# Rearranging the first 605 entries of a hand-kept instruction order (attention, token mixing, weight conversion)

## Chip, cores and metric

One Trainium2 chip, one of its cores. The metric is device time in microseconds (us), the median of the runs shown; lower is better.

## The reference

For a batch of 4, 8 heads, 576 positions and a head width of 64 the reference computes three stages one after another, all in float32 accuracy:

```
out_d     = softmax(scale * q_d k_d^T) v_d        # q, k, v averaged over 4 neighbours: 144 positions
out_local = softmax(scale * q k^T, |i-j| < 4) v   # a band of 7 keys
x  = repeat(out_d, 4) + out_local                 # heads side by side: 4 x 576 x 512
u  = x + (relu(x^T w_tok1) w_tok2)^T              # token mixing, hidden width 256
u  = u + relu(u w_ch1) w_ch2                      # channel mixing, hidden width 1536
th = u w_theta;  y = w_tok_r (u cos th) + w_tok_i (u sin th)
out = (u + y) + relu((u + y) w_ch)
```

The weights come as 64-bit floats and are converted on the chip.

## The kernel before, in words

Products are made exact enough by splitting a float32 value into a high part (rounded by ScalarE, ACT) and a low part (the rest, by VectorE, DVE), and adding three TensorE (PE) products (lines 135 to 139). A 64-bit weight is turned into these two parts by `converted` (lines 146 to 198): a DMA of the raw words, two ACT operations (L173, L174), three DVE operations (L176 to L186), an integer add on GpSimd (POOL, L190), the rounding on ACT (L192) and the subtraction on DVE (L194).

Nothing orders the work of attention, token mixing, channel mixing and conversion but one list, `ORDER` (lines 30 to 69). Each name in it is a generator, and each entry runs that generator to its next `yield`, which emits the instructions of one step:

```python
with tc.manual_schedule(engines={act.engine, dve.engine, pool.engine, pe.engine, nc.sync.engine}):
    for e in ORDER:
        name, _, times = e.partition("*")
        for _ in range(int(times or 1)):
            next(gens[name], None)
```

So the list fixes, for every engine and for the one queue of SyncE (SP) that issues all DMAs, the order of its own instructions. Between engines only data and buffers make one wait for another. In this text a step is written with its number from 0: F0:6 is the seventh entry F0. The names:

- **P n**: DMA of queries and keys of head pair n (16 pairs, 582 KB, tile qk, four buffers). **K n**: DVE, the sums over four neighbours (L368, L369). **W n**: four DMAs of the pair's values, tile vw, two buffers (L334). **V Q**: DMA of the values of a quad (two pairs), then three POOL sums (L345, L348, L351).
- **L n**: banded attention of a pair. L:0 PE mask (pairs 0 to 3 begin with 24, 12, 12 and 12 filler products, L280), L:1 PE scores (L480), L:2 DVE maximum and subtraction (L492, L493), L:3 ACT exponent, L:4 PE transposes (L505), L:5 ACT copies, L:6 PE product with vw (L515), L:7 DVE division into x (L529).
- **F Q**: pooled attention of a quad. F:0 PE scores (L381, needs K of both pairs), F:1 DVE maxima (L399, L407), F:2 ACT exponents, F:3 PE transposes (L424, L429), F:4 ACT copies, F:5 PE product (L440 to L447, needs V), F:6 DVE division (L451 to L454), F:7 two DMAs of the result to DRAM (tile od, L457), F:8 three DMAs back, four times over (tile xu, L463, L466).
- **A n**: DVE adds xu to x (L542). **T Q**: token mixing of a quad. T:0 ACT high part, T:1 DVE low part (L553), T:2 ACT, T:3 and T:4 PE first product, T:5 to T:8 PE second product. **E** and **U** take these products out of PSUM (U's last step writes uT to DRAM).
- **G0 to G6**: conversion of the token mixing's weights, six steps (DMA, ACT, DVE, POOL, ACT, DVE); T0:3 needs G0 to G2, T0:5 needs G3 to G6. **X0 to X7**: the same for the first third of the channel weights. **C i**: channel mixing of 384 positions: DMA of uT, ACT, DVE, then PE in eight steps of 12 products, C:3 to C:6 (first product, needs X0, X1, X4, X5) and C:7 to C:10 (second, needs X2, X3, X6, X7), with **H** and **O** taking them out. **I**: the constants.

The scores, transposes and products of L and F share two wide PSUM buffers, so a step that takes one waits until an earlier one is read.

Of the kernel before, what the change touches and what calls it, by code (L numbers as in the profile page):

```python
# [27 lines left out]


ORDER = """  # L30
G3 P0 G2 I*2 P1 G3 P4 G3 V0 P2 G3 K0 G3 G2 I G2 I L0*2 P3 K1 F0 W1 L0 F0 L1 L0 G3 F0 V0 L1*2 P5 V0 L2 W0 G2 K2 V0 G2
F0 G1 L1 V1 F0 L2 K3 G0 G6 K4 L0 F0 L0 L2 L1 G2 F1 L2 K5 L1 L0 F1 G1*2 F1 F0 V1 W3 L0 F1 G5 G0 L1 F0 G0 F1 G6 F2 L1
G0 P6 W2 G5 G6 L3 V1 F2 F0 V1 L3 G6 F2 F1 L3 G1 G4 F1 L2 P7 L5 L2 K6 L5 F1 G1 L3 A0 V2 X0 A1 L3 G1 T0 L5 G0 T0 L2 G2
F1 L3 G0 G4 F2 G5 T0*2 V2 X2 L2 G6 W5 F2 K7 V2 L4*2 E0.0*2 T0 L4 V3 V2 A2 L3 E0.1 L5 G4 L4 W4 L5 G6 L5 G4 L3 X2 F3
G5 P8 P9 A3 G4 F2 G5 E0.1 T1 G4 G5 T0 F2 V3 L4 F3 F2 T0 L4 V3 X2 F3 L6 V3 L6 X7 T0 P11 L6 X2 X0 F3 K8 U0.0 L6 T0 X2
X0 U0.0 F3 L4 U0.0 V4 K9 F2 F3 X0 L6 L4 L6 T1 F4 U0.1 X0 F3 T1 L5 U0.1 X0 T1 U0.1 F4 X7 X4 V4 F3 T1 X7 F4 W6 L5 X7
E1.1 F4 E1.0 E1.1 L8 V4 L8 X7 E1.0 X1 A4 F4 T1 P10 A5 T1 X2 T2 L8 T1 U1.0*2 T2 T1 U1.0 X1 F3 L7 X7 L7 T2 X1 T2 X4 X5
K10 X1 L8 L6 U1.1*2 L7 T2 E2.0 U1.1 W7 X4 L7 V4 X1 L7 F4 W9 L7 L6 X4 E2.1 E2.0 C0 E2.1 T2 X1 L8 K11 X5 L7 T2 X5 L8
W8 L9*2 L7 X5 P13 T2 P12 L9 L10 C0 A6 F5 X4 C0 U2.0 L10 U2.0 X5 U2.0 C0 X3 F5 X6 F4 F5 C0 A7 F4 L10 T3 X4 F5 L9 V5
T3 H0.1 L8 U2.1 F5 T2 H0.1 H0.0 K12 T3 L9 U2.1 X5 C0 L9 U2.1 K13 F4 X6*2 L10 T3 X3 W13 H0.0 X6 H0.2 F6 E3.0*2 V5 P14  # L40
T3 F6 V5 H0.2 F6 C0 V6 V5 L8 X3 E3.1 L9 H0.3 F5 E3.1 X3 W10 L9 F6 X3 F5 L10 V6 A9 T3 F5 T3 V6 U3.0 L10 K14 T3 V6
U3.0 X6 U3.0 T3 H0.3 X3 X6 L11*2 C0 L11 P15 U3.1*2 A8 F6 U3.1 C0 F5 T4 L11 L12 L10 O0.1 K15 C0 C1 W11 L10 O0.0 C0
T4*2 F7 O0.3 O0.2 L12 C1 O0.3 T4 L12 F7 L12 T4 C1 L11 E4.1 F6 L11 F7 L11 F6 C1 A10 W12 E4.0 L11 F6 F7 E4.0 A11 F7
L12 E4.1 C1 H1.0 T5 C2 F6 L13*2 H1.1 L12 H1.1 T4 T5 T4 U4.0 L13 C1 U4.0 H1.0 U4.0 L13 V7 T4 H1.2 T5 L13 L15 L13 T4
U4.1 L12 U4.1 L15 L12 W15 V7 C1 H1.2 A12 V7 U4.1 T5 H1.3 V7 H1.3 L13 E5.0 C1 L13 F7 C1 F7 E5.0 F7 L15 L14*2 A13 L15
C1 O1.0 L14 F7 O1.1 L14 T5 W14 C1 E5.1 C2 E5.1 T6 L14 L15 L14 T5 T6 T5 U5.0 C2 T5 U5.0 L15 U5.0 T5 O1.2 T6 O1.3*2
L15 L14 T6 U5.1 L14 U5.1*2 L15 T6 E6.0 A14 A15 C2 E6.1 C3 E6.0 T7 E6.1 T6 T7 H2.0 T6 U6.0 H2.0 T7*2 U6.0*2 C3 T6*2
T7 U6.1*2 E7.0 U6.1 C2 E7.1*2 E7.0 T7 H2.1*2 T7 U7.0 T7 U7.0*2 T7 C2*2 H2.2 U7.1 H2.2 U7.1 C3 U7.1 R0 X8 X17 H2.3
X11 H2.3 C2 X19 C2*2 X8 O2.1 X8 C2 O2.2 X8 O2.0 X11 C3 O2.3*2 X21 C3 H3.0 X19 H3.0 X19 X8 C3 X17 X8 X17 C4 H3.1 C3
H3.2*2 X17 H3.1 X19 X20 H3.3 X21 H3.3 C3 X11 X9 C3 C4 O3.0 X21 X17 X19 C3 C4 X21 C3 O3.2 X11 X21 X13 C4 O3.3 O3.1  # L50
X21 O3.3 X12 X17 X9 C4 X9 X20 X19 C4 X9 H4.0 X13 H4.0 X20 C5 C4 X15 H4.2 H4.1 X9 H4.1 X20 H4.2 H4.3 B2 X16 H4.3 C4
X9 X13 C4 C5 X13 X20 C4 O4.1 X12 X10 C5 X13 C4 O4.2 X12 B2 C5 O4.0 X12 X11 X13 C5 O4.3 H5.0 X20 X16 O4.3 X23 B2 C5
H5.1 X10 H5.0 X10 C5 H5.2 X12 X11 X10 H5.1 B2 H5.3 X14 X10 H5.3 J0 H5.2 X16 C5 M2.4 X23 X10 X16 X23 X15 C5 X18 C5
O5.1 X23 X22 B2 O5.2 O5.0 X12 X15 X14 C5 X23 X14 X16 M2.5 B2 O5.3 X14 X16 O5.3 R1 B2 X15 X40 X23 X18 X30 M2.6 B2 X18
M2.5 X18 B2 M2.8 X22 M2.8 X35 X22 M2.7 B2 X15 X14 M2.4 X22 M2.6 M2.9 X18 M2.7 B2 X15 X22 X33 X14 X40 X18 X40 X30 B0
X22 M2.10 X40 M2.11 M2.9 M2.11 M2.10 B2 X40 X36 X30 X35 B2 X35 X30 B0 X33 B0 X35 X24 B2 X33 X35 X38 X30 X40 X33 B0
X30 X28 B0 X38*2 X36 B0 X36 X38 X33 B2 X35 M0.4 X36 X39 X28 M0.4 X28 X29 X38 B0 X38 X28 B0 M0.7 X27 M0.5 X36 M0.5
M0.6 M0.7 X28 X36 B0 X39 M0.6 X39 M0.8 B0 X29 X33 X39 X28 M0.9 B0 M0.10 X27 M0.8 M0.9 M0.10 M0.11 B1 X27 X24 X37
X39*2 M0.11 B0 X24 B0 X24 B1 X27 X34 B1 X27 X25 B0 X24 N0.0 X27 X29 X34 N0.0 X29 B0 X34 X25 X31 X24 B1 N0.3*2 X25
N0.3 B1 M1.4 N0.1 X25 M1.4 N0.2 B1 X34 N0.3 M1.5 X37*2 B1 N0.2 X37 N0.2 B1 M1.7 X25 M1.7 X37 X32 M1.5 X26 X29 N0.0  # L60
B1 M1.6 X29 M1.6 X37 N0.1 B1 M1.9 N0.1 X31 M1.9 X31 M1.8 B1 X34 X32 M1.8 X31 X25 M1.11 B5 M1.10 J1 X26 M1.10 M1.11
B1 X26 X32 X26 B1 B5 X32 X26 B5 X32 B1 N1.0 N1.1*2 N1.0 N1.1 B1 B5 N1.3 X26 N1.2 N1.3 B5 X34 N1.3*2 B5 M5.5 N1.0
M5.4 B5 M5.6*2 M5.5 N1.2 B5 M5.4 N1.2 J2 B5*2 M5.9 M5.7 X31 M5.7 M5.8 M5.9 B5 M5.8 M5.10 N2.0*2 N2.3 M5.11 B4 M5.10
M5.11 B5 N2.3 N2.1 N2.3 B5 B4*2 B5 X31 N2.1 N2.2 X32 R2 N2.3 N2.0 N2.1 B4*2 N2.2*2 B4 Z B5 M4.4 M4.5 M4.6*2 M4.4
M4.5 B4*2 M4.7 J4 B4 M4.8 B4 M4.9 ZS M4.9 M4.8 ZS B4 M4.10 M4.7 ZS M4.11 B3 M4.11 M4.10 B4*2 N4.0 B3 B4 N4.1*2 B3
N4.1 B4 N4.2*2 B3 N4.3*3 B3 N4.3 N4.2 B3 N4.0*2 B3 M3.6 M3.4 M3.5 M3.4 ZS J5 B3 M3.7 ZS M3.7 ZS*2 B3 M3.5 M3.8 M3.6
M3.8 B3 N5.3 N5.2 N5.3 N5.1 N5.3 B3 M3.10 N5.1 M3.9 M3.10 M3.9 N5.1 N5.0 M3.11*2 B3 N5.3 N5.2 ZS N5.2 N5.0 B3 J3
N5.0 B3 N3.0*2 N3.1 N3.0 B3 N3.1 N3.2 N3.1 N3.2*2 N3.3*4
""".split()
# [1029 lines left out]
```

## Time and profile before

| | us |
|---|---|
| median of 3 runs | 690.69 (686.81 to 691.47) |
| the profiled execution | 689.01 |
| its span, first to last instruction | 687.2 |
| PE busy | 663.0 (96% of the span) |
| DVE busy | 472.0 |
| granted clock of PE, mean | 0.989 of full |

The profile is of one execution. In the rows below, a row of instructions has start, duration, engine, line, operation, output and input, count, and in brackets how long the engine stood idle before it and what ended that. A row of a stretch has the stretch, its length, busy time of PE, PE's weight loads, DVE, ACT and POOL (with counts), the granted PE clock, the mean busy share of the DMA engines and GB/s.

### The profile page before, as it was taken

The numbers are of one execution on the slowest core, as the hardware profiler recorded it, in microseconds if no ns is written. First come the engines' busy times: TensorE is split into PE (matmuls) and PEld (weight loads), VectorE is DVE, ScalarE is ACT, GpSimd is POOL, SyncE is SP. The second block draws the span as 40 slices with busy tenths as digits, with TensorE's granted clock in tenths as the row PEclk, the third lists the DMA queues.
The fourth block names the chain that finished last, engine by engine and source line by source line (L and its number), as shares of the span: only waits on it lengthen the run. The fifth ranks groups of instructions, "written<-read, shape, count | busy, mean of one in ns | idle before, by whom it ended". The sixth has DMA issues, their size and how long they took to land.

```text
span 687.2 us, 17270 instructions
## 1 busy us (share of the span) xinstructions
PE 663.0 (96%) x7368; PEld 634.5 (92%) x7368; DVE 472.0 (69%) x840; ACT 304.8 (44%) x594; POOL 96.8 (14%) x79
## 2 busy tenths in 40 slices
...
PEclk9979999999999999999999999999999999999999
...
GB/s 291 209 273 221 253 273 258 186 163 163 87 145 155 192 286 196 207 168 131 150 209 55 174 156 169 74 140 134 23 132 1 132 92 0 61 140 1 70 1 70
DMA packets 85612, 100.36 MB, mean 146 GB/s; under 512 B 44256, under 2 KB 65888, under 8 KB 85536
## 3 DMA queue, kind: packets, MB, share of 16 engines
...
q14 instruction: 18, 0.15, 0.1%
HBM read 74.34 MB, written 24.90 MB: 144 GB/s over the span
## 4 chain that ended last, share of the span: by engine, by line
PE 87%; DMA 5%; DVE 5%; ACT 1%; issue 1%; SPq 0%; POOL 0%; DVEq 0%; POOLq 0%; ACTq 0%
PE c L646 7%; PE c L138 7%; PE c L137 7%; PE c L649 7%; PE c L647 7%; PE c L139 7%; PE y L137 6%; PE y L138 6%; PE y L139 6%; PE th L138 2%; PE th L137 2%; PE th L139 2%; PE t L137 2%; PE t L138 2%; PE t L139 2%; PE o L515 1%
## 5 line engine op out<-in xcount | busy, mean ns | idle before, releaser
L190 POOL TENSOR_TENSOR ww<-ww,raw 128x512 int32<-128x512 int32 (+2 forms) x43 | 65.3, 1523 | 184.9 <-DVE ww L186 89.8
L662 ACT ACTIVATE g<-c 128x384 fp32r<-128x384 f32 x72 | 34.3, 492 | 105.0 <-PE c L139 89.9
L137 PE MATMUL y<-wrh,zh 128*128 128x288 f32 x256 | 75.0, 296 | 0.0
L138 PE MATMUL y<-wrl,zh 128*128 128x288 f32 x256 | 74.9, 296 | 0.0
L139 PE MATMUL y<-wrh,zl 128*128 128x288 f32 x256 | 72.8, 295 | 0.0
L665 DVE SCALAR_TENSOR_TENSOR g<-c,g 128x384 fp32r<-128x384 f32 x72 | 37.8, 550 | 45.8 <-ACT g L662 39.5
L673 DVE TENSOR_TENSOR ut<-c,ut 128x384 f32<-128x384 f32 x48 | 25.7, 548 | 38.4 <-PE c L649 29.8
L137 PEld LDWEIGHTS y<-wrh,zh 128*128 128x128 f32 x256 | 48.0, 188 | 0.0
L138 PEld LDWEIGHTS y<-wrl,zh 128*128 128x128 f32 x256 | 48.0, 188 | 0.0
L139 PEld LDWEIGHTS y<-wrh,zl 128*128 128x128 f32 x256 | 47.2, 188 | 0.0
L173 ACT ACTIVATE ww<-raw 128x512 f32<-128x512 f32 (+2 forms) x43 | 29.2, 679 | 27.2 <-DMA raw<-w_ch 11.6
L879 DVE TENSOR_TENSOR cx<-y,cx 128x288 f32<-128x288 f32 x32 | 14.6, 456 | 30.8 <-PE y L139 30.4
L174 ACT ACTIVATE raw<-raw 128x512 int32<-128x512 uint32 (+3 forms) x48 | 31.8, 663 | 0.0
L186 DVE SCALAR_TENSOR_TENSOR ww<-raw,ww 128x512 uint32<-128x512 uint32 (+2 forms) x43 | 30.6, 712 | 1.5
L137 PE MATMUL th<-thh,cxh 128*128 128x512 f32 (+1 forms) x92 | 31.6, 343 | 0.0
L138 PE MATMUL th<-thl,cxh 128*128 128x512 f32 (+1 forms) x92 | 31.6, 343 | 0.0
L139 PE MATMUL th<-thh,cxl 128*128 128x512 f32 (+1 forms) x92 | 31.2, 343 | 0.0
L132 ACT CAST cuh<-cx 128x288 fp32r<-128x288 f32 (+1 forms) x16 | 8.8, 553 | 49.0 <-DVE cx L879 49.0
L176 DVE TENSOR_SCALAR ww<-ww 128x512 f32<-128x512 f32 (+2 forms) x43 | 24.1, 560 | 5.5 <-ACT ww L173 5.3
L515 PE MATMUL o<-vw,plt 38*32 38x65 f32 x1280 | 17.9, 236 | 6.7 <-DVE pbuf L493 4.8
L515 PEld LDWEIGHTS o<-vw,plt 38*32 38x32 f32 x1280 | 15.3, 110 | 9.4 <-DVE pbuf L493 5.0
L178 DVE TENSOR_SCALAR ww<-ww 128x512 uint32<-128x512 uint32 (+2 forms) x43 | 22.5, 523 | 1.5
...
## 6 DMA issues: line engine op xcount, KB each, us to landing
...
```

Of the source, the lines that this page charges most:

```text
L137: pe.matmul(out, lh, rh, start=start, stop=False, skip_group_check=again)
L138: pe.matmul(out, lh, rl, start=False, stop=False, skip_group_check=again)
L139: pe.matmul(out, ll, rh, start=False, stop=stop, skip_group_check=again)
L174: act.activation(f, words[:, :, 0], AF.Copy, scale=2.0**-29)
L186: dve.scalar_tensor_tensor(out=wu, in0=words[:, :, 1], scalar=0xC0000000, in1=wu, op0=ALU.bitwise_and, op1=ALU.bitwise_or)
L190: pool.tensor_tensor(out=w.bitcast(I32), in0=w.bitcast(I32), in1=f, op=ALU.add)
L515: pe.matmul(o[r : r + 32, 5 * j + i // 2], pts[h : h + W, i // 2, r : r + 32], vw[h : h + W, g, :], start=True, stop=True,)
L646: pe.matmul(ps[:, 0:MIX], h[:, cb % 2, d], h1, start=cb == cbs[0], stop=False)
L647: pe.matmul(ps[:, 0:MIX], l[:, cb % 2, d], h1, start=False, stop=False)
L649: pe.matmul(ps[:, 0:MIX], weight[cb // 2][2][:, cb % 2, d], h2, start=False, stop=cb == cbs[-1])
L662: act.activation(h1, ps, AF.Relu)
L665: dve.scalar_tensor_tensor(out=h2, in0=ps, scalar=0.0, in1=h1.bitcast(F32), op0=ALU.max, op1=ALU.subtract)
```

## The change

The first 605 entries are put in another order; after them both lists are equal, entry for entry (other lines of the diff are only broken elsewhere). Each step occurs as often as before. The list's start, and further on the places of C0, C1 and the late W loads:

```diff
-G3 P0 G2 I*2 P1 G3 P4 G3 V0 P2 G3 K0 G3 G2 I G2 I L0*2 P3 K1 F0 W1 L0 F0 L1 L0 G3 F0 V0 L1*2 P5 V0 L2 W0 G2 K2 V0 G2
-F0 G1 L1 V1 F0 L2 K3 G0 G6 K4 L0 F0 L0 L2 L1 G2 F1 L2 K5 L1 L0 F1 G1*2 F1 F0 V1 W3 L0 F1 G5 G0 L1 F0 G0 F1 G6 F2 L1
-G0 P6 W2 G5 G6 L3 V1 F2 F0 V1 L3 G6 F2 F1 L3 G1 G4 F1 L2 P7 L5 L2 K6 L5 F1 G1 L3 A0 V2 X0 A1 L3 G1 T0 L5 G0 T0 L2 G2
-F1 L3 G0 G4 F2 G5 T0*2 V2 X2 L2 G6 W5 F2 K7 V2 L4*2 E0.0*2 T0 L4 V3 V2 A2 L3 E0.1 L5 G4 L4 W4 L5 G6 L5 G4 L3 X2 F3
...
+P0 I*2 P1 I L0 K0 L0 V0 L0 K1 F0 L1 G6 L1 F0 P2 G6 K2 G2 G4 L0 G6 F0*2 G4 V0 P3 L1 L0 G5 V0 G0 G4 G2 K3 F0 G1 P4 W0 L0
+L2 F1 L2 V0 L1 G0 G2 F0 F1 G1 L2 G1 F1 G2 G0 L1 G5 V1 L1 F0 G2 V1 L2 W1 K4 G0 G3 X2 L3 L0*2 G3 P5 L3 G5 L3 G5 G0 F0 F1
+W2 G2 G0 V1 P6 G2 F1 G5 L1 L3 K5 F2 G1 L1 F0 L2 P7 G6*2 F2 G5 V1 W3 X0 G3 L2 F1 A0 G3 L5 F2 F1 L5 G1 L3 G3 L3 L4 G6 A1
+G4 L4 T0 L5 V2 L2 G1 F1 T0 G4 T0 G4 V2 X5 G3 L4 F1 X0 V2 W4 L4 L2 T0 E0.0 L3 T0 K6 X2 L3 F2 V3 E0.1 K7 L6 F2 E0.1 E0.0
...
+U2.1 V5 K12 T3 L11 T3 K13 T3 X7 L11 L8 L9 E3.0 X5 E3.1 H0.0 X5 L10 E3.0 H0.1 X3 L10 X3 F5 W9 L8 U2.1 L11 V6 E3.1 F4 C0
+X3 F6 X6 T3 L9 C0 F6 F5 X6 X3 F6 H0.3 U3.0 X3 T3 P15 V6 H0.2 F6 X7 T3 L9 L11 F6 L13 U3.0 X7 L11 W10 F5 X6 H0.2 X6 U3.0
+V6 A8 T3 F6 X7*2 H0.3 X6 A9 L13 X7 C0 U3.1*2 T4 U3.1 L13 L12 C0 L13 P14 T4 L12 F6 O0.1 C0*2 O0.0 K14 C1 O0.3 L12 V7 C1
...
+K15 L15 W14 I T4 H1.1 L12 V7 L14 L15 L14 A11 T5 U4.0 T4 T5 T4 T5 F6 U4.0 L14 C1 H1.3 L12 H1.2 U4.0 T5 U4.1 V7 C2 L15
+W13 F7 T4 L12 T5 H1.3 L14 L13 E5.0 F7 L13 C1 F7 A13 U4.1 C1 C2 F7*2 E5.0 E5.1 L14 V7 O1.1 U4.1 A12 C1 T6 C1 T6 E5.1
```

## Rows read from the trace of the kernel before

**Rows 1.** The page: granted PE clock in 40 slices, tenths of full.
```profile
PEclk9979999999999999999999999999999999999999
```

**Rows 2.** Busy time by stretch, columns as told above.
```profile
0.00:46.90 46.90, 31.14 (x924) 22.53 (x924) 33.38 (x67) 22.25 (x54) 12.24 (x18) 0.93 0.80 258
46.90:62.00 15.10, 13.77 (x392) 11.60 (x392) 14.06 (x25) 9.52 (x24) 6.29 (x6) 0.76 0.74 216
62.00:131.00 69.00, 66.00 (x1652) 58.87 (x1644) 63.26 (x120) 45.48 (x107) 22.41 (x19) 1.00 0.76 244
131.00:216.00 85.00, 85.00 (x1457) 81.17 (x1458) 43.04 (x77) 35.24 (x75) 3.40 (x3) 1.00 0.42 139
```

**Rows 3.** The stretch of 43.9 to 54 us, columns as in rows 2.
```profile
43.90:54.00 10.10, 6.61 (x114) 5.63 (x115) 9.80 (x15) 6.47 (x14) 2.76 (x3) 0.50 0.91 285
```

**Rows 4.** Waits of PE in the first 110 us: total, times, longest.
```profile
PE o L515 <- DVE pbuf L493: 4.8, 1, 4.8
```

**Rows 5.** The chain that ended last, 28 to 46 us: start, length, what.
```profile
31.00 5.23 DMA od<-ods
...
37.60 5.95 DMA xu<-ot
...
43.66 1.57 DVE x L542 x2
```

**Rows 6.** SP's queue in time order, 18 to 33 us and around 91 us.
```profile
18.09 1.28 SPq L163 DMA_DIRECT2D raw<-w_tok  x2
28.42 2.09 SPq L334 DMA_DIRECT2D vw<-vloc  x4
...
31.00 0.62 SPq L457 DMA_DIRECT2D od<-ods  x1
...
91.06 4.17 SPq L334 DMA_DIRECT2D vw<-vloc  x8
```

**Rows 7.** Stretches of 2 us with loads queued, columns as in rows 2.
```profile
2.00:4.00 2.00, 2.00 (x9) 1.19 (x8) 0.00 (x0) 0.45 (x3) 0.29 (x1) 1.00 0.99 359
...
10.00:12.00 2.00, 1.60 (x15) 0.99 (x11) 1.94 (x5) 0.72 (x2) 0.34 (x1) 1.00 1.04 421
```

**Rows 8.** DVE in time order.
```profile
4.06 0.31 DVE L176 TENSOR_SCALAR raw<-raw 128x288 f32<-128x288 f32 x1 [3.20 <-ACT raw L173]
...
4.75 0.46 DVE L186 SCALAR_TENSOR_TENSOR raw<-raw 128x288 uint32<-128x288 uint32 x1
5.62 1.14 DVE L368 TENSOR_TENSOR qa<-qk 128x576 f32<-128x576 f32 x1 [0.41 <-DMA qk<-qkT]
6.80 0.46 DVE L369 TENSOR_TENSOR qkd<-qa 128x288 f32<-128x288 f32 x1
...
8.20 0.76 DVE L368 TENSOR_TENSOR qa<-qk 128x576 f32<-128x576 f32 x1
...
24.25 1.48 DVE L369 TENSOR_TENSOR qkd<-qa 128x288 f32<-128x288 f32 x1
...
46.89 1.48 DVE L553 TENSOR_TENSOR xl<-x,xh 128x1280 fp32r<-128x1280 f32 x1
```

**Rows 9.** PE in time order: F0:5, T0:3, L7:6, L11's scores, C0:7.
```profile
22.49 0.65 PE L440 MATMUL od<-vl,pts 128*32 128x260 f32 x8
...
23.52 0.30 PE L447 MATMUL od<-vs,pts 128*32 128x65 f32 x8
...
51.15 0.58 PE L137 MATMUL t<-xh,w1h 128*128 128x256 f32 x1
...
96.54 1.04 PE L515 MATMUL o<-vw,plt 38*32 38x65 f32 x80
...
130.02 0.91 PE L480 MATMUL s<-qk 64*32 64x38 f32 x80
130.86 0.44 PE L646 MATMUL c<-g,c20h 128*128 128x384 f32 x1
```

**Rows 10.** POOL in time order, V1's first sum.
```profile
24.00 1.41 POOL L345 TENSOR_TENSOR vd<-vd 128x650 f32<-128x650 f32 x1 [8.80 <-DMA vd<-vtok]
```

More of the change, by code (lines that the diff above doesn't have):

```diff
@@ L30 @@
 ORDER = """
-G3 P0 G2 I*2 P1 G3 P4 G3 V0 P2 G3 K0 G3 G2 I G2 I L0*2 P3 K1 F0 W1 L0 F0 L1 L0 G3 F0 V0 L1*2 P5 V0 L2 W0 G2 K2 V0 G2
-F0 G1 L1 V1 F0 L2 K3 G0 G6 K4 L0 F0 L0 L2 L1 G2 F1 L2 K5 L1 L0 F1 G1*2 F1 F0 V1 W3 L0 F1 G5 G0 L1 F0 G0 F1 G6 F2 L1
-G0 P6 W2 G5 G6 L3 V1 F2 F0 V1 L3 G6 F2 F1 L3 G1 G4 F1 L2 P7 L5 L2 K6 L5 F1 G1 L3 A0 V2 X0 A1 L3 G1 T0 L5 G0 T0 L2 G2
-F1 L3 G0 G4 F2 G5 T0*2 V2 X2 L2 G6 W5 F2 K7 V2 L4*2 E0.0*2 T0 L4 V3 V2 A2 L3 E0.1 L5 G4 L4 W4 L5 G6 L5 G4 L3 X2 F3
-G5 P8 P9 A3 G4 F2 G5 E0.1 T1 G4 G5 T0 F2 V3 L4 F3 F2 T0 L4 V3 X2 F3 L6 V3 L6 X7 T0 P11 L6 X2 X0 F3 K8 U0.0 L6 T0 X2
@@ L36 @@
[L36 to L65, printed above, removed]
@@ L66 @@
-N4.1 B4 N4.2*2 B3 N4.3*3 B3 N4.3 N4.2 B3 N4.0*2 B3 M3.6 M3.4 M3.5 M3.4 ZS J5 B3 M3.7 ZS M3.7 ZS*2 B3 M3.5 M3.8 M3.6
-M3.8 B3 N5.3 N5.2 N5.3 N5.1 N5.3 B3 M3.10 N5.1 M3.9 M3.10 M3.9 N5.1 N5.0 M3.11*2 B3 N5.3 N5.2 ZS N5.2 N5.0 B3 J3
-N5.0 B3 N3.0*2 N3.1 N3.0 B3 N3.1 N3.2 N3.1 N3.2*2 N3.3*4
+P0 I*2 P1 I L0 K0 L0 V0 L0 K1 F0 L1 G6 L1 F0 P2 G6 K2 G2 G4 L0 G6 F0*2 G4 V0 P3 L1 L0 G5 V0 G0 G4 G2 K3 F0 G1 P4 W0 L0
+L2 F1 L2 V0 L1 G0 G2 F0 F1 G1 L2 G1 F1 G2 G0 L1 G5 V1 L1 F0 G2 V1 L2 W1 K4 G0 G3 X2 L3 L0*2 G3 P5 L3 G5 L3 G5 G0 F0 F1
@@ new lines @@
+W2 G2 G0 V1 P6 G2 F1 G5 L1 L3 K5 F2 G1 L1 F0 L2 P7 G6*2 F2 G5 V1 W3 X0 G3 L2 F1 A0 G3 L5 F2 F1 L5 G1 L3 G3 L3 L4 G6 A1
+G4 L4 T0 L5 V2 L2 G1 F1 T0 G4 T0 G4 V2 X5 G3 L4 F1 X0 V2 W4 L4 L2 T0 E0.0 L3 T0 K6 X2 L3 F2 V3 E0.1 K7 L6 F2 E0.1 E0.0
+A2 L5 L6 L4 T0 L6 P9 L4 F3 A3 L6 P8 T1 F3 U0.0 P11 V3 X0 T0 V2 F2 T1 L5 U0.0 L5 T0 F2 T0 V3 K8 W5 F3 U0.0 V4 U0.1*2 L4
+F3 T1 L4 F3 T1 X0 L6 F2 L5 L6 K9 X1 V3 F2 X0 F4 U0.1 X2 L5 T1 X0 F4 V4 E1.0 F3 L8 X2 W6 E1.0 E1.1 X1 L8 E1.1 F4 T1 A5
+W7 U1.0 L8 T1 U1.0 L7 A4 T1 L7 X1 T2 V4 X2 T2 X4 L7 T1 P10 T2 U1.0 K10 F4 T2 U1.1*2 F3 X2 L6 L8 U1.1 F4 L7 V4 V5 K11
@@ new lines @@
+L6 F3 L8 T2 X1*2 E2.0 X1 L8 X5 F5 E2.1 X4 E2.1 F4 E2.0 L7 C0 T2*2 F5 F3 L7 X5 L9*2 F5 L7 U2.0 T2 X4 L9 V5 T2 L7 P12 W8
+V5 P13 C0 X4 U2.0 C0 U2.0 X3 F5 W11 V6 F4 A6 L10*2 F5 A7 X4 L10 L9 X4 X5 T3 C0 L11 T3 F4 C0 L10 H0.0 U2.1 L9 H0.1 X6
+U2.1 V5 K12 T3 L11 T3 K13 T3 X7 L11 L8 L9 E3.0 X5 E3.1 H0.0 X5 L10 E3.0 H0.1 X3 L10 X3 F5 W9 L8 U2.1 L11 V6 E3.1 F4 C0
+X3 F6 X6 T3 L9 C0 F6 F5 X6 X3 F6 H0.3 U3.0 X3 T3 P15 V6 H0.2 F6 X7 T3 L9 L11 F6 L13 U3.0 X7 L11 W10 F5 X6 H0.2 X6 U3.0
+V6 A8 T3 F6 X7*2 H0.3 X6 A9 L13 X7 C0 U3.1*2 T4 U3.1 L13 L12 C0 L13 P14 T4 L12 F6 O0.1 C0*2 O0.0 K14 C1 O0.3 L12 V7 C1
```

23 lines of the change are left out of this document (added).

## Prediction

> **What bounds the kernel now.** I read the page first, then busy time by stretch, then the waits of PE and DVE, and last the chain and the engines' own order up to 131 us. In the page the reader is to see a PE clock below full only near the start [rows 1]. By stretch, PE is busy all of 85.0 us from 131 to 216, while DVE needs only 43.0 there [rows 2]; past 216 both lists are equal. So the end is PE's total work plus whatever PE stands idle, or runs slowly, before it is saturated. That loss is in front: 15.8 us idle up to 46.9, 1.3 up to 62, 3.0 up to 131 (each stretch less PE's busy time) [rows 2]. It also runs at half clock, granted 0.50, from 43.9 to 54, in which 6.6 us were busy; at full clock that work takes half, so some 3.3 us are lost there [rows 3]. No order can win more than these 23 us and the remaining scraps of half clock.
>
> Why PE stands idle: its longest wait is one of 4.8 us for DVE's subtraction in L:2 [rows 4]. It ends a chain, not DVE's work: F0:7 sends the pooled result of quad 0 to DRAM at 31.00, it takes 5.2 us to land, the way back starts at 37.60 and takes 5.95, and only at 43.66 can DVE run A0 [rows 5]. L5:2, which frees the PSUM buffer that PE wants for L2:6, stands behind A0 and A1 on DVE. F0:7 itself is late through SP's queue: W3 stands ahead of it and waits for a vw buffer, that is for L1:6, so SP issues nothing from 19.4 to 28.42 [rows 6]. DVE is the second limit: between 46.9 and 131 it is busy 77.3 of 84.1 us [rows 2].
>
> **The change, part by part.** No step is added or removed, so every engine's sum of work stays. What counts is which steps stand ahead of two points: T0:1 with T0:3, the first token mixing, and C0:7, from which PE works without a gap.
>
> *The first loads.* P0 is now the first DMA; before, G3's 288 KB went first and the sums of K0 began at 5.62 [rows 8]. Those bytes take 0.8 us at the 359 GB/s of 2 to 4 us [rows 7], so K0 begins near 4.8. DVE waits 4.8 us in place of doing G3's step first.
>
> *F0 on DVE.* Ahead of F0:6 the new list drops G3:2, G3:5, G2:5, K4, K5 (4.5 us) and puts in G6:2, G4:2, G0:2 (3.8 us); a 288-wide conversion step is 1.1 us (4.06 to 5.21), a K some 1.25 without its wait (0.76 at 8.20, plus 0.46) [rows 8]. Listed DVE work up to the end of F0:6 is 18.2 us. Its waits I work out by walking the list: 4.8 for P0; 2.2 where L0:2 stands before K1 and its scores end near 8.3 behind the 24 fillers; 0.6 each for F0's and F1's scores. With 0.7 for operations that POOL stretches, F0:6 ends at 27.1.
>
> *SP past F0:7.* W3 now stands behind F0:8, and the entries ahead of F0:7 wait only for early readers (the last, P5, for K1 and L1:1). So the issue at 31.00 becomes 27.2. If the way from there to A0 takes the same 12.66 us (43.66 less 31.00) [rows 5], A0 starts at 39.9. Listed DVE work ahead of A0 is 29.3; with 8.2 of waits and 1.3 of stretching DVE is there at 38.8, so only 1.1 is waited, in place of 2.9.
>
> *T0.* From A0 to T0:1 stand 4.7 us of DVE, so T0:1 starts near 44.8; before at 46.89 [rows 8]. Ahead of T0:1 the new list has 2.1 us more of DVE's work done (G4:2, G5:2, G0:5, G5:5, G6:5 in, G3:5 and K6 out). PE now goes straight from T0:1's end at 46.3 to T0:3, because F2:3 stands behind T0:4; before it began at 51.15 [rows 9]. PE's work ahead of T0:3 is the same to 0.15 us (F2:3 out, L4:0 and L4:1 in). That is a lead of 4.7 us.
>
> *T0 to C0:7, by PE.* Ahead of C0:7 the new list has four PE steps more: L11:4 at 0.65, L13's mask and scores at 1.1 (scores 0.91 [rows 9]), F6:5 at 1.3 (F0:5 took 22.49 to 23.82 [rows 9]), in all 3.0. They are work, not loss: C0:7 itself may come later by that and nothing is lost. If PE loses on this way what it loses now (4.3 us idle from 46.9 to 131 [rows 2], and the half clock), the lead stays 4.7.
>
> *The same way by DVE.* Ahead of C0:7 DVE's work is the same to 0.7 us (L11:2, A8 in, K14 out). From T0:1 on it is 77.3 + 0.7 - 2.1 = 75.9 us, with today's 6.8 of idle 82.7, so C0:7 at 44.8 + 82.7 = 127.5; now 130.86 [rows 9]. With the 3.0 of PE work more done by then, DVE would allow a lead of 3.4 + 3.0 = 6.4.
>
> *Later.* From C0:7 on PE has DVE far ahead (43.0 of 85 us [rows 2]), which hides X7's late conversion and the other moved steps. If X7:5 is late, all of C0's second product waits; its DVE work is in the 75.9.
>
> *Unknown prices.* The PE clock: if the new list's sparse PE up to 46 us keeps T0 at half clock as now, nothing changes; if it stays full, up to 3.3 us more are won; one more such stretch loses as much. I take nothing, the row's own state, and keep both ends. The two ways give 4.7 by PE, 6.4 by DVE; I take 5.0, near PE's, as PE sets the end. From the profiled 689.01 (span 687.2 and 1.8 around it) that is 684.0. The median of the runs shown, 690.69, lies 1.7 above that execution; I state 685.0 between 684.0 and 685.7.
>
> **POOL and DVE.** K5's second sum at 24.25 takes 1.48 us in place of 0.46 [rows 8], while POOL's L345 runs from 24.00 to 25.41 [rows 10]. The new list has two of POOL's adds more ahead of T0:1, G4:3 and G5:3. The Trainium skill, SBUF — State Buffer, section "Who interferes with whom", says that a VectorE instruction with two SBUF inputs contends with a GpSimd instruction that reads SBUF. By that rule, which this row bears out, two adds at 0.8 us each could take 1.6 off, and the sum would be 3.4 in place of 5.0.
>
> **The rivals.**
>
> *More is won (B).* DVE's count (6.4) holds, not PE's, and part of the half clock goes: 8 us, so 681. For it: a PE that starts T0 earlier with more conversions done may have smaller gaps up to 131. Against: my walk leaves out small handoffs.
>
> *Nothing is won at the front (C).* Ahead of F0:7 the new list has queued 8.75 MB. At the mean 258 GB/s up to 46.9 [rows 2] these take 34 us, and the result of F0 would go behind them, land near 39 and be back at 46.5, so A0 is 2.9 later than now and T0:1, 4.7 behind it, starts at 51.2; T0:3 at 52.7 is 1.6 later than now, and the time is 690.6. Against: that mean holds the stretch in which SP stood still; while loads were queued, 359 and 421 are read [rows 7], and at 360 the 8.75 MB are done by 26.
>
> *Slower (D): the values come late where PE is saturated.* At L9 and L13 the new list leaves one vw buffer free (W11 and W14 hold the other early), so W9 cannot be issued before L8:6, nor W13 before L12:6. From there to L9:6 and L13:6 PE has 5.7 and 5.3 us of other work; before, the least such distance in that part is some 10. W7, the first half of eight issues from 91.06 [rows 6], had landed by L7:6 at 96.54 [rows 9], 5.5 us later, so each wait lies between 0 and, behind an xu load of 5.95 us [rows 5], some 6. I take 0. Two full waits make 12 less the 5 won: 696. It turns the sign once both together pass 5 us.
>
> **How the numbers follow.** My case (won 2 to 6.9) 0.51, B 0.26, C 0.14, D 0.09. A measurement of this kernel can tell about 1%, 6.9 us, from no change. B is faster by over 1%, and 0.03 of my case's upper end with it: 0.29. D is slower: 0.09. The rest, 0.62, lies within 1%. My case's own range is 682 to 687; the range to state goes to B's 681 less the other 2 us of clock, 679, and to C's 690.6 with a measurement's spread, 692. Outside are D and the far end of B.
>
> **What would show it.** Right: the DMA of od at L457 first issued near 27 us, A0 near 40, T0's first product near 46, no wait of PE above 3 us behind DVE's L493, the PE steps from 131 on without a gap, idle time of PE to 131 near 15 us in place of 20. Wrong: F0:7 issued by 28 but xu back after 43 (C); PE idle before L515 near 110 or 145 us with SP's L334 just ahead (D); granted clock 0.50 over more than 10 us; or DVE idle more than 12 us in all before T0:1.

## The result, and the profile after

The changed order is slower: 694.23 us against 688.15 (medians of 16 runs each), a ratio of 1.0078 with a 95% interval of 1.0056 to 1.01. One run of after took 1287.33 us and is left out of the ratio, as is one slow run each of e5 and e11 below. That is 5.4 us more where 5 less were forecast, and above the range stated. The profiled execution took 696.35 us, 2.1 above its median, and its span is 694.6; before they were 689.01 and 687.2.

First the page of after: busy time by engine, the granted clock in 40 slices, and one of the DMA queues. It answers to [rows 1].

```profile
PE 668.0 (96%) x7368; PEld 638.3 (92%) x7368; DVE 470.1 (68%) x840; ACT 304.8 (44%) x594; POOL 99.3 (14%) x79
...
PEclk9868999999999999999999999999999999999999
...
q8 instruction: 58, 0.95, 0.6%
```

The same 7368 products take 5.0 us more of PE's time (663.0 before), and the clock's first four slices are lower. DVE's sum is smaller by 1.9: in this execution the two more adds of POOL cost DVE nothing.

Next the stretches of [rows 2], of after: length, PE, PE's weight loads, DVE, ACT, POOL, clock, DMA share, GB/s.

```profile
0.00:46.90 46.90, 31.97 (x958) 23.46 (x959) 33.43 (x73) 25.69 (x64) 14.62 (x20) 0.87 0.89 276
46.90:62.00 15.10, 14.31 (x384) 12.97 (x364) 12.13 (x21) 6.51 (x14) 5.33 (x4) 0.61 0.68 233
62.00:131.00 69.00, 64.54 (x1612) 56.94 (x1611) 56.67 (x108) 42.30 (x102) 21.91 (x17) 0.98 0.70 221
131.00:216.00 85.00, 82.83 (x1453) 77.68 (x1452) 46.35 (x83) 34.53 (x74) 6.56 (x6) 1.00 0.41 137
```

Length less PE's busy time gives the idle time: 14.9, 0.8, 4.5 and 2.2 us, where before had 15.8, 1.3, 3.0 and 0. So the front wins 0.9 us, not 4.7, and PE now has gaps where it had none, past 131 us. The first two clocks, 0.87 and 0.61, say that much of the early work ran at half clock.

Which waits are these? PE's own waits of after: total, times, longest (after's lines are numbered one lower than before's).

```profile
PE s L479 <- issue: 6.9, 3, 5.7
PE s L476 <- DVE pbuf L492: 2.5, 1, 2.5
PE pt L504 <- DVE pbuf L492: 2.1, 2, 1.4
...
PE pt L504 <- ACT pts L432: 1.7, 1, 1.7
PE t L136 <- issue: 1.5, 1, 1.5
PE pdt L423 <- issue: 1.3, 1, 1.3
...
PE c L136 <- issue: 0.8, 1, 0.8
```

The 4.8 us of [rows 4] are gone, as forecast. At the top stands "issue": PE waited for no data, no buffer and no engine that the profile shows. The same view of before has this row too, and the prediction left it out:

```profile
PE s L480 <- issue: 4.6, 3, 3.1
```

The longest "issue" wait of after, among PE's instructions in time order (start, duration, line, tiles, count, idle time before):

```profile
27.31 0.64 PE L479 MATMUL s<-qk 64*32 64x38 f32 x44
33.60 0.51 PE L479 MATMUL s<-qk 64*32 64x38 f32 x31 [5.66 <-issue]
```

It cuts the 80 products of L3's scores in two, after the 49th. They all have the same operands and buffers, so no data can be the cause: the sentence ahead of the prediction that between engines only data and buffers make one wait leaves out a wait of this kind. DVE stood behind these scores (DVE in time order):

```profile
34.21 0.55 DVE L491 TENSOR_REDUCE mx<-s 128x10 f32<-128x380 f32 x1 [2.91 <-PE s L479]
...
41.76 0.82 DVE L541 TENSOR_TENSOR x<-x,xu 128x640 f32<-128x640 f32 x1
```

Its last row is A0, without a wait ahead of it. What is special about the 49th product? Count PE's records in order of time: products, weight loads, and the 111 semaphore and drain instructions of its sequencer. The wait (5.86 us from the last start before it to the first behind it, as the waits by "issue" are measured from here on) lies after record 1217, and the others after 1729, 1985, 3521, 4801, 5569 and 7361: all are 256 k less 63, with whole k. In before the waits by "issue" lie after 449, 705, 961, 4289 and 4801, the same ladder. In all 17 traces of this case the profile names 115 waits of PE by "issue", and 111 of them stand at 256 k less 63; the other four are of 0.3 us. So PE's instructions arrive in blocks of 256, and PE waits when it has used one up before the next is there. The page's queue row supports it: 58 transfers of 16 KB, and after's 14847 records by 256 are 58.0. Ahead of four of after's waits PE had used a block fast, because steps with many small products stand together (L:1 with 80 in 0.9 us, L:6 with 80 in 1.0): the block took 1.26 us ahead of the wait at 27.75, and 3.8, 2.75 and 2.8 us ahead of those at 105.2 (1.53 us), 121.6 (0.91) and 164.9 (1.76). Over all traces 59 of the 78 blocks used up in under 4 us ended in such a wait, 37 of the 196 that took 4 to 5 us, and 15 of the 682 longer ones. The Trainium skill, "Runtime: NRT & Kernel Launch", section "Instruction fetch mechanics", gives the block of 256 instructions and calls the cost of crossing one mostly hidden; the ladder agrees with the first, the waits of up to 5.9 us are against the second.

The second loss is another wait. ACT, SP and PE of after around 90 us:

```profile
89.69 0.70 ACT L599 COPY us<-t 128x256 f32<-128x256 f32 x2 [2.15 <-DMA uT<-us]
```
```profile
83.21 7.53 SPq L602 DMA_DIRECT2D uT<-us  x2
```
```profile
91.84 0.77 PE L504 MATMUL pt<-fixed,pbuf 128*128 128x128 f32 x5 [1.70 <-ACT pts L432]
```

U1.1's copies need the only us buffer back, from which U1.0's transfer reads until 89.6. In the new list they stand ahead of F4's copies on ACT, and PE waits for these. Then the stretches at half clock, 31.2 to 38.0 from within the long wait, 44.9 to 58.5 around T0, and 92.7 to 96.1 behind this one (columns as above):

```profile
31.20:38.00 6.80, 4.40 (x148) 3.48 (x150) 3.57 (x8) 2.12 (x6) 4.10 (x5) 0.50 0.74 227
44.90:58.50 13.60, 11.48 (x274) 10.45 (x274) 11.22 (x20) 6.08 (x11) 3.23 (x3) 0.50 0.79 271
92.70:96.10 3.40, 3.40 (x41) 3.10 (x45) 2.22 (x6) 2.73 (x8) 0.28 (x1) 0.50 0.87 257
```

With a fourth stretch, 10.8 to 14.2, they make 27.3 us at half clock; before had 13.7. To compare runs I add up stretches of 2 us from 0 to 222: idle is length less PE's busy time, the clock's loss is busy time times one less the granted clock.

| one execution of | idle | lost to the clock | span | span less both |
|---|---|---|---|---|
| before | 20.1 | 4.9 | 687.2 | 662.2 |
| after | 22.3 | 11.4 | 694.6 | 660.9 |
| e5_old256 | 19.7 | 7.7 | 689.0 | 661.6 |
| e6_old128 | 28.6 | 13.7 | 704.6 | 662.3 |
| e11_u11 | 15.7 | 11.8 | 688.9 | 661.4 |
| e13_oldw3 | 16.9 | 9.8 | 688.9 | 662.2 |
| e15_oldu11 | 19.3 | 4.0 | 685.7 | 662.4 |

The last column stays within 2 us here (in the other runs it reaches 664.8): PE's work is fixed, and the time is what these two columns make of it. After against before: 2.2 idle and 6.5 clock, 8.7, for a span 7.4 longer. One execution is not the median, though: e5 and e15 keep before's list up to 85 us and more, and lose 7.7 and 4.0 to the clock.

### The profile page after: what moved, and what is told of

It is laid out like the page before. It is cut to its first block, busy times and chain, and to the rows that moved or that the text cites. A ratio compares the mean times of both kernels' runs of the same rounds, so it can differ in the third digit from the quotient of the medians.

```text
span 694.6 us, 17278 instructions
## 1 busy us (share of the span) xinstructions
PE 668.0 (96%) x7368; PEld 638.3 (92%) x7368; DVE 470.1 (68%) x840; ACT 304.8 (44%) x594; POOL 99.3 (14%) x79
## 4 chain that ended last, share of the span: by engine, by line
PE 89%; DMA 5%; DVE 2%; issue 2%; ACT 1%; SPq 0%; DVEq 0%; ACTq 0%
PE c L645 7%; PE c L136 7%; PE c L646 7%; PE c L648 7%; PE c L137 7%; PE c L138 7%; PE y L136 5%; PE y L137 5%; PE y L138 5%; DMA raw<-w_tok 3%; PE t L136 3%; PE th L136 2%; PE th L138 2%; PE th L137 2%; PE o L514 2%; PE t L138 2%
## 5 line engine op out<-in xcount | busy, mean ns | idle before, releaser
L672 DVE TENSOR_TENSOR ut<-c,ut 128x384 f32<-128x384 f32 x48 | 25.7, 548 | 39.6 <-PE c L648 30.8
L172 ACT ACTIVATE ww<-raw 128x512 f32<-128x512 f32 (+2 forms) x43 | 29.2, 679 | 27.1 <-DMA raw<-w_ch 9.3
L878 DVE TENSOR_TENSOR cx<-y,cx 128x288 f32<-128x288 f32 x32 | 14.6, 456 | 31.0 <-PE y L138 30.6
L138 PE MATMUL th<-thh,cxl 128*128 128x512 f32 (+1 forms) x92 | 31.2, 343 | 0.0
L131 ACT CAST cuh<-cx 128x288 fp32r<-128x288 f32 (+1 forms) x16 | 8.8, 552 | 49.2 <-DVE cx L878 49.2
L175 DVE TENSOR_SCALAR ww<-ww 128x512 f32<-128x512 f32 (+2 forms) x43 | 22.5, 524 | 4.5 <-DMA raw<-w_ch 2.2
L136 PE MATMUL t<-w2h,h 128*128 128x256 f32 (+1 forms) x64 | 21.5, 336 | 1.5 <-issue 1.5
L479 PE MATMUL s<-qk 64*32 64x38 f32 x1280 | 16.1, 213 | 6.9 <-issue 6.9
```

The lines of the kernel that those rows point to most:

```text
L136: pe.matmul(out, lh, rh, start=start, stop=False, skip_group_check=again)
L138: pe.matmul(out, ll, rh, start=False, stop=stop, skip_group_check=again)
L172: act.activation(w, high, AF.Abs)
```

## The experiments

The lists are given in step notation, a few entries around each move. Each ratio is to runs of before made beside that run; after itself was not run again beside them.

**Front or rest?** Two mixed lists: the new front (144 entries, to T0:3) with the steps that are left in the old order, and the reverse.

```diff
-new list
+e1: new list's first 144 entries, then all other steps in the old order
+e2: old list's first 140 entries, then all other steps in the new order
```

> The new list's first 144 entries (up to T0:3), then all others in the old order. Theory F (the loss is made in front, by PE's waits for its own instructions while the DMA queue is full, and by the half clock that follows): slower than before by 4 to 6 us. Theory R (the loss is made by the order behind T0): within 1.5 us of before.

> The old list's first 140 entries (T0:3 is the 127th), then all others in the new order. Theory F: within 1.5 us of before. Theory R: slower than before by 5 to 7 us.

Measured: e1 1.0053 (1.0019 to 1.0087), e2 1.0103 (1.0066 to 1.014). Neither theory has it alone: the front wins nothing by itself, and the two losses, 0.5 and 1.0%, do not add up to after's 0.8. Where the order behind T0 costs, the traces show: from the start of T2:3's last product to C2:7, between which the same work is done, it takes 124.7 us in before and 125.6 in e1 with the old order, 132.4 in after and 132.5 in e2 with the new one. The wait after record 7361 is absent with the old rest (before, e1) and there with the new one (1.76 us in after, 1.69 in e2); e2 also waits 1.92 after 4801, where e1 does not wait for a block.

**A thinner front, and a shifted count.** In e3 two large loads leave the stretch in which the long wait lies. In e4 pair 3 loses its 12 fillers, 24 PE instructions ahead of L3's scores.

```diff
-G3:0 X2:0 L3:0
+G3:0 L3:0
...
-V1:2 P6:0 G2:6
+V1:2 G2:6
...
-F0:8 L2:4
+F0:8 P6:0 L2:4
...
-X0:0 G3:2
+X0:0 X2:0 G3:2
```
```diff
-WARM = [24] + [12] * 3 + [0] * 12
+WARM = [24] + [12] * 2 + [0] * 13
```

> The new list with two loads issued later: X2:0 (512 KB) behind X0:0, and P6:0 (582 KB) behind F0:8. If PE's 5.7 us gap within L3:1 is a wait for instructions behind queued loads, it shrinks below 3 us and the time falls by 3 to 6 us below the new list's. If the gap has another cause it stays at 5 to 6 us, and the time within 1.5 us of the new list's.

> The new list without the 12 filler products of pair 3: PE's instruction stream is 24 shorter from there on. If the gap stands at a count of PE's instructions (a multiple of 256, less 63 that the records lack), it moves 12 products further, from the 50th of L3:1's 80 to the 62nd, at the same count 1217. If it belongs to L3:1's data, it stays at the 50th or goes. The fillers' 1.8 us are not the question.

Measured: e3 1.0072 (1.0035 to 1.0108), e4 one execution at 695.73 us. e3 did not win the 3 to 6 us. Its wait among L3's scores, after the same record, is half as long as after's, but that is no sign of the loads: in e1, e9 and e11, whose lists are after's up to there, the same wait is 2.0 to 2.3 us. e4's stands 12 products further on (PE in time order, of e3 and e4):

```profile
31.69 0.50 PE L479 MATMUL s<-qk 64*32 64x38 f32 x31 [2.81 <-issue]
```
```profile
28.93 0.33 PE L479 MATMUL s<-qk 64*32 64x38 f32 x5
...
29.00 0.28 PE L479 MATMUL s<-qk 64*32 64x38 f32 x3
...
29.04 1.00 PE L479 MATMUL s<-qk 64*32 64x38 f32 x53
32.01 0.46 PE L479 MATMUL s<-qk 64*32 64x38 f32 x19 [1.97 <-issue]
```

In e4 61 products run ahead of it, where after has 49: 12 products fewer ahead of it move the wait by 12 products. The place is set by the count, not by the data.

**The same list, another place in the block.** The fillers ahead of pair 0's mask are cut into more and narrower products, so that the columns stay nearly the same and all later steps move along the count. M is the number of products added: e5 128 (a whole block, the control), e6 64, e7 92, e8 40. For e5:

```diff
-        warm(s[:, 0, 192:512], WARM[n])
+        warm(s[:, 0, 192:242] if n == 0 else s[:, 0, 192:512], 152 if n == 0 else WARM[n])
```

> The list of before; the 24 filler products of 320 columns ahead of pair 0's mask become 152 of 50 columns: nearly as many columns, 128 products (256 PE instructions) more. Control for the next run. Theory P (what counts is where PE's instruction count passes the multiples of 256): all later steps keep their place in a block, so the time stays, within 0.3%, and the waits behind T0 are those of before (one of 0.6 near 102 us). Theory Q (PE's waits come from data, buffers and the order alone): also within 0.3%. If the narrow products themselves cost something, it shows here.

> The list of before; the 24 fillers become 88 of 86 columns: nearly as many columns, 64 products (128 instructions) more, so every later step stands half a block further on; order and data are untouched. By the records of before, the blocks then used up in under 4.3 us fall short of it by 17.0 us in all, in place of 2.6; past 50 us they are reached near 51, 93, 96, 117, 135, 158 and 183 us. Theory P: new waits of PE for nothing in the profile, 0.5 to 3 us each, at most of these, idle time 5 to 12 us more and the time 0.6 to 1.5% longer than before. Theory Q: same time as the control, within 0.3%.

> The list of after; the 24 fillers become 116 of 66 columns: 92 products (184 instructions) more. By the records of after the shortfall below 4.3 us a block goes from 7.1 to 3.9, and no block past 70 us falls short. Theory P: the waits at 105, 122 and 165 us go, the time is 2 to 4 us less than after's (ratio to before near 1.003, from 1.001 to 1.006). Theory Q: ratio as after's, 1.008.

> The list of after; the 24 fillers become 64 of 120 columns: 40 products (80 instructions) more. By the records of after the shortfall goes from 7.1 to 16.4, with short blocks ahead of 42, 72, 94, 127 and 153 us. Theory P: waits at these places, 4 to 9 us more than after, ratio to before 1.013 to 1.021. Theory Q: ratio as after's, 1.008.

Measured: e5 1.000 (0.998 to 1.0021); e6 1.024 (1.0201 to 1.0278); e7 1.0095 (1.0071 to 1.0119); e8 1.0103 (1.0073 to 1.0132). The old list, half a block further on, is 17 us slower with not one step moved. PE's waits of e6, and one of them in time order with the products behind it:

```profile
PE o L514 <- issue: 6.3, 4, 2.5
PE s L479 <- issue: 5.3, 2, 3.2
...
PE od L446 <- issue: 1.9, 1, 1.9
```
```profile
173.72 0.84 PE L479 MATMUL s<-qk 64*32 64x38 f32 x68
176.69 0.35 PE L479 MATMUL s<-qk 64*32 64x38 f32 x7 [2.13 <-issue]
...
177.46 0.52 PE L137 MATMUL c<-ul,c11h 128*128 128x384 f32 x1
177.78 0.52 PE L138 MATMUL c<-uh,c11l 128*128 128x384 f32 x1
```

Behind the wait two products of 384 columns start 0.32 us apart; in before at 175.00 and 175.17 such products start 0.17 apart. That is the half clock, granted 0.50 from 176.4 to 179.8, and it adds to the price of the wait: 2.33 idle and 1.6 for the clock. It follows three of e6's waits past 100 us (at 107.6, 174.4 and 203.2, of 3.4, 2.3 and 2.7 us). So e6 has 8.5 us more of idle time than before and 8.8 more lost to the clock (6.0 more than the control e5), twice what the expectation had from the waits alone. Of the seven places forecast past 50 us six waited (at 57, 104, 108, 133, 174 and 203; before passes the same counts at 58, 100, 103, 124, 165 and 190, so the times named were some 7 us early, and what is left is what had been lost until then); the block forecast for 135 did not, and one at 78.6 waited that had not been forecast.

e7 and e8 went against the expectation: neither became 2 to 4 us faster nor 4 to 9 slower, and both intervals hold the 1.008 of theory Q. By their times these two runs do not support theory P; the places of their waits do. In e7 the waits past 70 us did shrink (0.5, 0.4 and 0.8 at 100.9, 110.5 and 149.8), but the front met other blocks, and T0:3's last product starts at 59.4 in place of 53.0. From T2:3's last product to C2:7 e7 takes 126.9 us, after 132.4, before 124.7. In e8 four of the five forecast places waited (at 51.7, 82.3, 102.6 and 139.2, later than named as in e6), the one for 153 did not, and its idle time is 23.3 where after has 22.3. Moving the count heals one place and hurts another.

**Breaking the bunches.** e9 puts 12 long products of channel mixing (2.1 us) into two bunches. e10 puts L3:0's fillers between two.

```diff
-X3:2 F5:5 W9:0
+X3:2 C0:5 F5:5 W9:0
...
-L15:1 L14:1 A11:0
+L15:1 C1:6 L14:1 A11:0
```
```diff
-L3:0 L0:6 L0:7
+L0:6 L3:0 L0:7
```

> The list of after with two moves: C1:6 (12 products, 2.1 us) now stands between the scores of L15 and L14, and C0:5 between L10:4 and F5:5. Theory P (PE waits where 128 products are used up in under some 4 us at the end of an instruction block): the blocks that took 2.75 us (ahead of 121.6) and 2.82 us (ahead of 164.9) now take near 5, so the waits of 0.91 and 1.76 go or fall below 0.4; with nothing else changed 2.5 us less than after, ratio near 1.004 (1.002 to 1.007). Theory Q (the order's data and buffers cost the time): waits of the same size remain at other steps, ratio 1.008.

> The list of after with one move: L3:0 (12 fillers of 320 columns and the mask, some 1.9 us) stands behind L0:6 in place of ahead of it. The count of PE instructions ahead of L3:1 stays, but the last 128 products ahead of the wait at 27.75 us now hold the fillers and take near 3.1 us in place of 1.26. Theory P: the wait of 5.86 us falls by the difference, to some 4, T0 starts 1 to 2 us earlier, time 1 to 2 us less than after (ratio 1.004 to 1.008). Rival: the block arrives when the loads in the DMA queues let it, whenever PE gets there: PE comes to the boundary at the same time as before, the wait ends at the same moment, and the time stays (1.008).

Measured: e9 1.0056 (1.0032 to 1.0081), e10 1.0086 (1.0054 to 1.0119). e9's wait at 121.6 is gone but the next block, now without C0:5, waits 1.53 at 123.3, in the middle of L8's values; that before T4:7 fell from 1.76 to 1.00:

```profile
124.81 0.34 PE L514 MATMUL o<-vw,plt 38*32 38x65 f32 x13 [1.31 <-issue]
...
163.97 0.22 PE L479 MATMUL s<-qk 64*32 64x38 f32 x1 [0.80 <-issue]
```

The gain of 0.2% is inside the intervals, and the waits at blocks past 50 us add up to 4.5 us where after has 4.9. In e10 the wait in L3's scores is gone, where theory P had some 4 us left, and T0 is later all the same: two waits of 1.8 and 1.6 us stand at 22.6 and 27.2, and F0:6 comes at 30.8 in place of 26.4.

**U1.1's copies.** They go behind F4's copies on ACT.

```diff
-U1.1:0 U1.1:1 F3:6 X2:5 L6:6 L8:3 U1.1:2 F4:4 L7:3
+F3:6 X2:5 L6:6 L8:3 F4:4 U1.1:0 U1.1:1 U1.1:2 L7:3
```

> The list of after with U1.1's three steps behind F4:4 (F3:6, X2:5, L6:6, L8:3, F4:4 go ahead of them), so that ACT no longer waits for the transfer of U1.0's result with F4's copies queued behind. If the wait of 1.70 of PE at 91.8 us comes from there and the stretch at half clock from 92.6 to 96.0 from that wait: both go, 1.7 idle and 1.7 of clock, and the time is 2 to 3.4 us less than after (ratio 1.003 to 1.005). If PE is held by something else there, or the gain is lost at the next instruction block: 1.008.

Measured: 1.0027 (1.0004 to 1.005), where after has 1.0078: 3.5 us back from one move, the most of any run on the new list. The stretch 90 to 110 of e11, and of after (columns as above):

```profile
90.00:110.00 20.00, 20.00 (x531) 17.98 (x529) 19.44 (x35) 14.46 (x33) 6.84 (x5) 1.00 0.89 273
```
```profile
90.00:110.00 20.00, 17.05 (x441) 15.00 (x427) 17.42 (x35) 13.34 (x32) 6.99 (x5) 0.91 0.83 261
```

PE is busy all of it at full clock, 531 products in place of 441. The wait of 1.53 us at 105.2, too, is gone. From T2:3's last product to C2:7 it takes 126.6 us; two waits at 116.4 (0.93) and 159.8 (1.57) are left, and before's 124.7 is 1.9 below. The 3.5 us are of the medians; single executions differ. The wait for F4's copies, 1.70 in after, is 1.5 to 1.6 in e2 and e9, 0.3 to 0.7 in e3, e8 and e10 and absent in e4 and e7, all with U1.1 where after has it, and e11's profile loses as much to the clock as after's, in front.

**Together, in the other direction, and SP alone.** e12 has e3, e9, e10 and e11 at once, e14 e3, e11 and C1:6 of e9. e13 is the old list with W3:0 moved past F0:7 alone. e15 puts U1.1's wait into the old list.

```diff
-V1:1 W3:0 L0:7
+V1:1 L0:7
...
-F0:7 G0:2
+F0:7 W3:0 G0:2
```
```diff
-L7:1 T2:2
+L7:1 U1.1:0 U1.1:1 T2:2
...
-L6:6 U1.1:0 U1.1:1 L7:2
+L6:6 L7:2
```

> The list of after with the moves of the three runs before and the later X2:0 and P6:0 of the thinned front. Theory P and the sums of the single runs: front wait of 3 or less, no waits at 121.6 and 164.9, no half clock near 94: 6 to 9 us less than after, 685 to 688, ratio 0.995 to 1.000. If the single gains do not add up because other blocks are then used up fast, or because the half clock comes elsewhere: 690 to 693, ratio 1.002 to 1.006.

> The list of before with W3:0 alone moved from ahead of F0:7 to directly behind it: the one part of the change by which SP is no longer held. F0:6 ends at 29.02 in before, so od is sent near 29.5 in place of 31.0. By the prediction's step 1.5 us are won at A0 and T0, and with nothing else moved the time is 1 to 1.5 us less (ratio 0.998). Rival (the DMA queue): the loads that W3 held back now run ahead of and beside od's way and PE's instruction blocks, the gain is eaten and the ratio is 1.000 to 1.003.

> The list of after with X2:0 and P6:0 later (thinned front), U1.1 behind F4:4 and C1:6 between the scores of L15 and L14. If the single gains add up (thinned front 0.5 to 3 us, U1.1 3.5, C1:6 0.7 against after's ratio of 1.0078): ratio 0.997 to 1.001, that is, the changed order is then no worse than before. If the gains go into other instruction blocks or half clock, as in the run with all four repairs: 1.003 to 1.005.

> The list of before with U1.1's two copies moved ahead of T2:2, directly behind U1.0's transfer. Theory (an ACT step that needs the one us buffer back stands ahead of ACT work that PE is waiting for): the copies wait on ACT some 4 us for the transfer sent at 85.2, T2:2 and with it T2:3 are late by about as much, PE stands idle 2 to 4 us near 88 and then runs 3.4 us at half clock (1.7 us lost): 3.5 to 6 us longer, ratio 1.005 to 1.009. If PE has enough other work there, or catches up before it is saturated: within 0.2%.

Measured: e12 1.0043 (1.0016 to 1.007), e13 1.0029 (0.9999 to 1.006), e14 1.0035 (1.0018 to 1.0053), e15 1.0019 (0.9997 to 1.004). No version beats before.

The repairs do not add up: e12 and e14 still wait at blocks, at other places (e14: 3.1 us at 28.3, 1.8 at 48.2 and at 104.3). e15 is a miss for its theory; what came is the other case it named, that PE has enough other work there. The copies do wait, 2.5 us, but PE only 1.1 for T2:2 behind them, at full clock:

```profile
87.21 0.70 ACT L599 COPY us<-t 128x256 f32<-128x256 f32 x2 [2.50 <-DMA uT<-us]
```
```profile
88.67 0.38 PE L564 MATMUL t<-xs,w1s 128*128 128x256 f32 x1 [1.09 <-ACT xs L556]
```

So such a wait on ACT costs by what PE has left to do beside it: in the new list 1.7 us, half clock and the block behind it, in the old one nothing that the runs can tell.

e13 is the cleanest test of the prediction's first steps. SP sends od at 27.28 (before 31.00, [rows 6]), A0 comes at 40.55 (43.66 before, [rows 5]), T0:1 at 43.78 and T0:3's last product at 51.0, these three 3.1 us earlier than in before's profile. Part of that is scatter: in e15 and e2, which have before's front unmoved, T0:1 comes at 44.91 and 45.83, so W3's place is worth 1 to 3 us there. At T2:3 2.5 of the 3.1 are left, at C0:7 none: C0:7 starts 1.7 later than before. PE, SP and ACT of e13 there:

```profile
102.43 0.69 PE L136 MATMUL c<-uh,c10h 128*128 128x384 f32 x1 [1.05 <-ACT us L599]
```
```profile
92.82 0.39 SPq L618 DMA_DIRECT2D ut<-uT  x1
```
```profile
100.12 1.47 ACT L625 CAST uh<-ut 128x1536 fp32r<-128x1536 f32 x1 [4.50 <-DMA ut<-uT]
```
```profile
102.40:109.30 6.90, 6.55 (x19) 6.15 (x20) 6.66 (x12) 4.54 (x11) 0.00 (x0) 0.51 0.78 262
```

The first product of channel mixing waits for ACT's copies to us, which stand behind uh on ACT, and uh waits for C0's first load, sent 2.6 us earlier than in before (95.45) but landed after 7.3 us; uh starts only 0.9 earlier (100.98 before). PE came early, waited, also for a block (1.06 at 99.5), and then ran 6.9 us at half clock.

## Why the prediction was wrong, step by step

*The first loads, F0, SP past F0:7: right.* F0:6 ended at 26.9 (27.1 forecast) and od was sent at 26.93 (27.2). So close is in part luck: in e1, e9 and e11, with the same front, F0:6 ended at 26.6 to 29.2. By e13 the step past F0:7 is worth 1 to 3 us at T0.

*A0 at 39.9: wrong by 1.9, and not by the way of od.* SP's queue of after, which answers to [rows 6], and A0 in before, to be held against after's row above:

```profile
26.93 0.62 SPq L456 DMA_DIRECT2D od<-ods  x1
...
34.33 0.62 SPq L462 DMA_DIRECT2D xu<-od  x1
```
```profile
43.66 1.56 DVE L542 TENSOR_TENSOR x<-x,xu 128x640 f32<-128x640 f32 x2 [2.92 <-DMA xu<-ot]
```

The way out took 7.4 us, where before took 5.23 [rows 5]; from 27.7 to 33.6 the DMA engines were busy 0.94 of the time, and the prediction had taken the dense queue as done by 26. But in after A0 does not wait for it: DVE comes to A0 straight from a conversion step, at 41.76. What failed is "DVE is there at 38.8". Ahead of A0 DVE was idle for 13.3 us, where the walk had 8.2 of waits, and busy for 28.5, where it had 30.6. Of the idle time 2.91 us are for L3's scores, that is, for a block of instructions; the walk had no term for that and left out the row that carries it, "PE s <- issue". In all eleven profiles with the new front A0 has no wait; in the six with the old one it waits 1.2 to 3.4 us for xu. Where that wait is shorter, stretching can take its place: in e9 (A0 at 42.90) DVE was busy for 32.4 us ahead of A0, with two steps of G that took 0.55 and 0.68 us in after and 2.68 here, beside POOL's add:

```profile
34.07 2.68 DVE L193 TENSOR_TENSOR w1l<-raw,w1h 128x256 fp32r<-128x256 f32 x2
```
```profile
34.72 1.48 POOL L189 TENSOR_TENSOR raw<-raw 128x512 int32<-128x512 int32 x1
```

So the prediction's term for it, 1.3 us, was too small for such an execution, and its paragraph on POOL and DVE has the right mechanism.

*T0:3 at 46.3: wrong by 3.8.* From A0 to T0:1 it took 4.9 us (4.7 forecast), so A0's delay came through whole: T0:1 at 46.70. Then T0:3 did not follow "straight from T0:1's end": PE was busy at half clock with scores and values that stand ahead of it, and waited 0.8 for a block; it began at 50.06. The lead over before's profile was 1.1 us, not 4.7, and over several profiles there is none: T0:3 begins at 48.9 to 50.5 with the new front (after, e1, e9, e11) and at 49.2 to 51.2 with the old (before, e2, e15).

*"If PE loses on this way what it loses now": this failed.* From T2:3 to C2:7 it lost 7.7 us more, and e2 lost as much with the old front. Named by the runs: U1.1's copies ahead of F4's on ACT (3.5 us with what follows from it, by e11), and the blocks ahead of 121.6 and 164.9, 2.7 us of waiting, of which the runs could take away only a part without making another. The blocks' price holds from execution to execution: the waits of over 0.35 us at blocks between 50 and 220 us add up to 4.5 to 5.1 us in the six profiles after, e2, e3, e9, e10 and e14, and to 0.6 to 1.1 in the five with the old order there (before, e1, e5, e13, e15). e6 shows by its time that the place in the blocks costs by itself; that these 4 us are part of after's loss is read from the traces, and no run took them away. The prediction checked buffers of vw and of PSUM for the moved steps but not the one us buffer, and it did not count how many small products stand together.

*"I take nothing" for the clock: wrong by 6.5 us in these two profiles.* The ends were kept (3.3 either way) for one stretch at T0; but in after stretches stand at other waits too (31.2 and 92.7), the second of a kind that the row of before could not show since PE had none past 54 us. How much of the 6.5 is the order's is open, since e5 lost 2.8 more than before with before's list.

*The rivals.* D did not come: PE waits nowhere before L514 near 110 or 145. C's mechanism came in part, the way of od took 2.1 us longer, but A0 did not wait for it. That its price would be paid behind T0, in a part taken as fixed, no rival said. Of the signs named ahead, "granted clock 0.50 over more than 10 us", gaps past 131 us and DVE idle for more than 12 us before T0:1 (13.5, as in before) came true against the forecast, and idle time to 131 us stayed at 20.2 us where near 15 was named; "no wait above 3 us behind DVE's L493" held.

*Open.* Which part of the front costs the 0.5% of e1 the runs do not settle: in single profiles the front scatters by some 2 us even where two lists are equal (F0:6 starts at 26.4 in after, 28.7 in e9). Why a block comes late is open too. That data fill the DMA engines was not tried by itself, and the waits at 121.6 and 164.9 came with them busy only 0.23 and 0.39 of the 5 us around.
